# A fused retention and Mish-MLP kernel on one core: the first tile's q and k in pair loads with products in place of transposes

## The chip, the cores and the metric

The kernel runs on one NeuronCore of one Trainium2 chip. The metric is the device time of one execution in microseconds, as a median over runs. Engines are named PE (TensorE), ACT (ScalarE), DVE (VectorE), POOL (GpSimd) and SP (SyncE). SP's queue issues loads and stores without a cast; POOL's queue issues loads that may cast f32 to bf16 on the way.

## What is computed

For 8 batches of 8 heads with 576 tokens of 64 elements, a retention: scores of q and k, scaled and multiplied by a decay that depends on the head and on the distance of two tokens, zero where the key comes later, and then multiplied by v. The result, laid out as 4608 tokens of 512 elements, goes through a two-layer network whose activation is Mish.

```python
scores = scale * np.matmul(q, k.transpose(0, 1, 3, 2))
Dmat = np.where(rel >= 0, gamma[:, None, None] ** rel[None, :, :], 0.0)
ret = scores * Dmat[None, :, :, :]
attn = np.matmul(ret, v)
x = attn.transpose(0, 2, 1, 3).reshape(B * S, H * D)
h = x @ w_in                       # [4608, 512] @ [512, 2048]
g = h * np.tanh(np.log1p(np.exp(h)))
out = g @ w_out                    # [4608, 2048] @ [2048, 512]
```

All inputs and the output are f32 in DRAM; the kernel computes products in bf16 with f32 sums.

## The kernel before

The tokens are cut into 36 chunks of 128, four to a tile, so there are nine tiles of 512 tokens. Tiles 0 and 1 hold the first chunk of each batch (batches 0 to 3, and 4 to 7), which need no running state. For every tile, `g1` forms one 128-wide slice of h with four products of 512 columns and ACT applies Mish to it (16 slices a tile), and `g2` multiplies by w_out. PE works its instructions off in the order in which they are written; the whole order is written out by hand, and each engine keeps it. Attention work of later tiles is put between the products of earlier ones. Only tile 0 has nothing to hide behind: its attention is the opening, from the start to the first `g1` product.

The opening, and the names that the change touches:

- **Loads of q and k.** In tiles 0 and 1 a partition holds eight consecutive tokens of one head (16 groups of eight tokens times 8 heads are 128 partitions, 512 elements each), so that one DRAM row is 2 KB long. `load_first_qk(t, i, b)` (line 100) loads one batch from POOL's queue with a cast to bf16. For tile 0, q of batches 0 and 1 is instead loaded by SP's queue in f32 to `q0` (lines 118 and 119) and cast by DVE (lines 510 and 511). The order on POOL's queue is k of batches 0 and 1, then, after the setting up of the distance matrix and the positions, k and q of batches 2 and 3, then v of all four batches in two loads (`load_first_v`), then w_in in pieces of 256, 256 and 512 columns (`load_w_in`, line 84). The two last pieces of 512 columns are issued later, behind the casts of v that POOL does (lines 521 and 530).
- **Transposes.** `f_transpose(t, g, i, parts)` (line 179) works on two batches, g = 0 or 1, and on q (i = 0) or k (i = 1). For tile 0 it makes 16 PE transposes (a token slot r out of eight, times two batches x) of 64 columns of the loaded tile with all 128 partitions, eight to a PSUM tile, and two evictions (`parts` names the PSUM pool and the engine of each) bring them to `qkT`, with the slots interleaved back into token order. Tile 1 first mixes the two batches with DVE (`f_mix`) and makes eight transposes.
- **Scores, v, outputs.** `f_scores(0, g)` makes 16 products and four masked evictions by DVE (line 217). `f_v` casts v to bf16 with the engine that it is given. `f_out(0, b, engine)` makes 8 products and one eviction to `xT`, which `g1` reads.
- **Warmers.** `keep_warm(n)` issues n products of zeros, whose result is not used.
- **Behind the opening.** POOL goes on with tile 1's q and k, w_out and `f_state`; `f_mix` and `f_transpose(1, 0, ...)` follow the 64 products of `g1(0, ...)`.

The written order of the opening (lines 510 to 533) stands in the listing.

Of the kernel before, what the change touches and what calls it, by code (L numbers as in the profile page):

```python
# [9 lines left out]
F32 = mybir.dt.float32  # L10
BF16 = mybir.dt.bfloat16
# [5 lines left out]
def kernel(  # L17
# [18 lines left out]
    nc = tc.nc  # L36
    B, H, S, D = q.shape
    assert (B, H, S, D) == (8, 8, 576, 64)
    P = 128
    NP = H // 2  # L40
    d_model = H * D
    d_ff = moe_w_in.shape[1]
    nF = d_ff // P
# [22 lines left out]
    tr = ctx.enter_context(tc.tile_pool(name="tr", bufs=4))  # L66
# [4 lines left out]
    ps_sc = ctx.enter_context(tc.tile_pool(name="ps_sc", bufs=2, space=PS))  # L71
    ps_st = ctx.enter_context(tc.tile_pool(name="ps_st", bufs=1, space=PS))
    ps_h = ctx.enter_context(tc.tile_pool(name="ps_h", bufs=2, space=PS))
# [10 lines left out]
    def load_w_in(f0, n):  # L84
        nc.gpsimd.dma_start(out=w_in_t[:, :, ds(f0, n)], in_=w_in_r[:, :, ds(f0, n)])
# [7 lines left out]

    stage = gp.tile([P, nF, NCH * P], BF16, name="gT")
    gts = {0: gp.tile([P, nF, NCH * P], BF16, name="gT")}
    q0 = gts[0][:, H:nF, :].bitcast(F32).rearrange("p (b a) c -> p b (a c)", a=2)
    v0 = {}
    fst = {}

    def load_first_qk(t, i, b):  # L100

        name = ("qb", "kb")[i]
        if t not in fst:
            fst[t] = {"qb": stage[:, 0:4, :], "kb": stage[:, 4:8, :], "vb": {}}
        nc.gpsimd.dma_start(out=fst[t][name][:, b, :],  # L105
                            in_=(q, k)[i][4 * t + b, :, 0:P, :].rearrange("h (g r) d -> g h (r d)", r=8))

    def load_first_v(b):

        if b < 4:  # L110
            pair = stage[:, ds(8 + 2 * b, 4), :].bitcast(F32).rearrange("p a (c d) -> p (a c) d", d=D)
        else:
            pair = first.tile([P, 2 * H, D], F32, name="vpair", bufs=2)
        for e in range(2):
            v0[b + e] = pair[:, ds(H * e, H), :]
        nc.gpsimd.dma_start(out=pair, in_=v[ds(b, 2), :, 0:P, :].rearrange("b h p d -> p (b h) d"))  # L116

    for b in range(2):
        nc.sync.dma_start(out=q0[:, b, :], in_=q[b, :, 0:P, :].rearrange("h (g r) d -> g h (r d)", r=8))
    for b in range(2):  # L120
        load_first_qk(0, 1, b)

    zeros = consts.tile([P, 512], BF16)
    nc.vector.memset(zeros, 0.0)
# [7 lines left out]
    ident = consts.tile([P, P], BF16)  # L132
# [3 lines left out]
    nc.gpsimd.iota(pos[64:P, 4:5], pattern=[[1, 1]], base=512, channel_multiplier=1,  # L136
                   allow_small_or_imprecise_dtypes=True)
    for i in (1, 0):
        for b in (2, 3):
            load_first_qk(0, i, b)  # L140
    load_first_v(0)
    load_first_v(2)
    for f0, n in ((0, 256), (256, 256), (512, 512)):
        load_w_in(f0, n)
    mask = consts.tile([P, P], F32)
    mask2 = consts.tile([P, P], F32)
# [13 lines left out]
    def keep_warm(n, pool=ps_o, name="ops"):  # L160
        idle = pool.tile([P, 512], F32, name=name)
        for _ in range(n):
            nc.tensor.matmul(idle, lhsT=zeros[:, 0:P], rhs=zeros, start=True, stop=True)
# [8 lines left out]
    def f_mix(g, i):  # L172
# [3 lines left out]
        nc.vector.tensor_copy(fst[1][name, "mix", g].rearrange("p r x d -> p x r d"),  # L176
                              fst[1][name][:, ds(2 * g, 2), :].rearrange("p x (r d) -> p x r d", r=8))

    def f_transpose(t, g, i, parts):

        name = ("qb", "kb")[i]
        out_t = tr.tile([P, 2, NP, P], BF16, name="qkT", bufs=5).rearrange("p i n t -> p (i n) t")
        n = 8 // len(parts)
        moves = []
        for j, (pool, tname, copy) in enumerate(parts):
            tp = pool.tile([P, 2, 8, P] if tname == "sc" else [P, 8, P], BF16, name=tname)
            tp = (tp[:, 0] if tname == "sc" else tp)[:, 0:n]
            for r in range(n):
                if t == 1:
                    mix = fst[1][name, "mix", g][:, n * j + r]  # L190
                    nc.tensor.transpose(tp[:, r, :], mix.rearrange("p x d -> p (x d)"), ident)  # L191
                else:
                    for x in range(2):
                        nc.tensor.transpose(tp[ds(64 * x, 64), r, :],
                                            fst[0][name][:, 2 * g + x, ts(n * j + r, D)], ident)
            moves.append((copy, out_t.rearrange("p h (g r) -> p h g r", r=8)[:, :, :, ds(n * j, n)],
                          tp.rearrange("p r (g h) -> p h g r", h=H)))
        for copy, to, src in moves:
            copy(to, src)
        fst[t][name, g] = out_t  # L200

    def f_scores(t, g):

        qT, kT = fst[t]["qb", g], fst[t]["kb", g]
        scs = [ps_sc.tile([P, 2, NP, P], F32, name="sc") for _ in range(2)]
        for x in range(2):
            fst[t]["sm", 2 * g + x] = first.tile([P, H, P], BF16, name="sm0", bufs=4)
        for hs in (0, NP):
            for h in range(hs, hs + NP):
                for x in range(2):  # L210
                    r = ds(64 * x, 64)
                    to = scs[hs // NP][:, x, h - hs, :] if t == 0 else scs[x][:, hs // NP, h - hs, :]
                    nc.tensor.matmul(to, lhsT=kT[r, h, :], rhs=qT[r, h, :], start=True, stop=True)
            for x in range(2):
                sm = fst[t]["sm", 2 * g + x]
                if t == 0:
                    nc.vector.tensor_tensor(sm[:, ds(hs, NP), :], scs[hs // NP][:, x], dmask[:, ds(hs, NP), :],
                                            op=OP.mult)
                elif hs > 0:
                    nc.vector.tensor_tensor(sm, scs[x].rearrange("p a b i -> p (a b) i"), dmask, op=OP.mult)  # L220

    def f_v(t, b, copy):
        vb = first.tile([P, H, D], BF16, name="vb", bufs=4)
        copies = copy if isinstance(copy, tuple) else (copy,)
        n = H // len(copies)
        for j, copy in enumerate(copies):
            copy(vb[:, ds(n * j, n), :], v0[4 * t + b][:, ds(n * j, n), :])
        fst[t]["vb"][b] = vb

    def f_out(t, b, copy):  # L230
        if b == 0:
            xts[t] = xp.tile([P, KC, NCH * P], BF16, name="xT")
        vb = fst[t]["vb"][b]
        if t == 0:
            pool, name = ((ps_h, "hp"), (ps_h, "hp"), (ps_st, "st"), (ps_o, "ops"))[b]
            ot = pool.tile([P, NP, P], F32, name=name)
        else:
            ot = ps_sc.tile([P, 2, NP, P], F32, name="sc")[:, 0]
        for p in range(NP):
            for e in range(2):  # L240
                nc.tensor.matmul(ot[ds(64 * e, 64), p, :], lhsT=vb[:, 2 * p + e, :],
                                 rhs=fst[t]["sm", b][:, 2 * p + e, :],
                                 start=(p == 0), stop=True, skip_group_check=True)
        copy(xts[t][:, :, ts(b, P)], ot)
# [256 lines left out]
    dve, act, pool = nc.vector.tensor_copy, nc.scalar.copy, nc.gpsimd.tensor_copy  # L501
# [5 lines left out]
    nc.scalar.activation(gq, ex, AX.Exp)  # L507
    nc.scalar.activation(gv, ex, AX.Exp, scale=-1.0)
    nc.scalar.activation(warm, lnd, AX.Mish)
    for b in range(2):  # L510
        dve(fst[0]["qb"][:, b, :], q0[:, b, :])
    keep_warm(12)
    f_transpose(0, 0, 1, [(ps_h, "hp", act), (ps_h, "hp", dve)])
    f_transpose(0, 0, 0, [(ps_st, "st", act), (ps_o, "ops", dve)])
    keep_warm(2, ps_sc, "sc")
    f_transpose(0, 1, 1, [(ps_h, "hp", act), (ps_h, "hp", act)])
    f_scores(0, 0)
    f_transpose(0, 1, 0, [(ps_st, "st", act), (ps_o, "ops", act)])
    for b in range(2):
        f_v(0, b, pool)  # L520
    load_w_in(1024, 512)
    keep_warm(3, ps_h, "hp")
    f_scores(0, 1)
    keep_warm(3)
    f_out(0, 0, act)
    f_out(0, 1, act)
    keep_warm(4, ps_st, "st")
    f_v(0, 2, dve)
    f_v(0, 3, (act, pool))
    load_w_in(1536, 512)  # L530
    f_out(0, 2, dve)
    f_out(0, 3, act)
    keep_warm(2, ps_sc, "sc")
    for i, b in ((1, 0), (1, 1), (0, 0), (0, 1)):
        load_first_qk(1, i, b)
# [9 lines left out]
    for b in (4, 6):  # L545
        load_first_v(b)
# [17 lines left out]
    for i in range(nF):  # L564
        for step in steps.get(i, "").split():
            n = int(step[1])
# [27 lines left out]
    for u in range(24):  # L594
        j, w = divmod(u, 4)
# [33 lines left out]
    for t in range(2, nT + 1):  # L629
        for i in range(nF):  # L630
            n, w = NCH * (t + 1) + i // 8 * 2, i % 8
# [84 lines left out]
```

## Time and profile before

| | |
|---|---|
| runs before | 305.67 us median of 3 (305.58 to 305.85) |
| the profiled execution | 305.06 us |
| its span in the profile | 303.3 us, 6347 instructions |
| opening: first product of g1 (line 435) | at 16.60 us |
| the 64 products of g1 for tile 0 | 16.60 to 30.83 us |
| data moved | 47.35 MB, mean 156 GB/s; HBM read 38.80 MB |

The 40 slices of the span show the shape of the run (each digit is a busy share in tenths):

```profile
PE   7899999999999999999999999999999999999996
DVE  4713546678969737363666463636271511011011
ACT  5556227883466534334343333434433333333200
POOL 8786857847966465561939392716210000000000
DMA  7999999999999969699999896979322100010131
```

PE is short of nine tenths in the first two slices (to 15.2 us) and in the last. The DMA engines are at nine tenths for more than half of the run. The groups of loads that concern the opening (queue, count, KB each, median time from issue to landing; for a casting load the KB are those written):

```profile
w_in_t<-in_moe_w_in_dram POOLq DMA_DIRECT2D x3, 512.0 KB, 10.5
gT<-in_k_dram POOLq DMA_DIRECT2D x8, 128.0 KB, 6.3
gT<-in_v_dram POOLq DMA_DIRECT2D x2, 512.0 KB, 7.0
gT<-in_q_dram POOLq DMA_DIRECT2D x6, 128.0 KB, 8.6
gT<-in_q_dram SPq DMA_DIRECT2D x2, 256.0 KB, 3.9
w_in_t<-in_moe_w_in_dram POOLq DMA_DIRECT2D x2, 256.0 KB, 8.0
```

`gT` is the name of the buffer that the opening borrows for its loads.

### The profile page before, as it was taken

How to read it: one execution, taken by the hardware profiler on the slowest of the kernel's cores; microseconds unless marked ns; L12 is line 12 of the kernel's file. 1: busy time of each engine (PE TensorE's matmuls, PEld its weight loads, DVE VectorE, ACT ScalarE, POOL GpSimd, SP SyncE). 2: the span in 40 equal slices, each digit the busy share in tenths (PEclk: the TensorE clock that was granted, in tenths of full speed). 3: DMA queues.
4: the chain of work that ended last, by engine and by line, in shares of the span. 5: the costliest groups of instructions: out<-in, count | busy, mean ns of one | idle time of the engine just before them, and what ended most of it. 6: DMA issues, size and time to landing. Idle time of an engine off the chain costs nothing.

```text
span 303.3 us, 6347 instructions
## 1 busy us (share of the span) xinstructions
PE 297.0 (98%) x2682; PEld 147.4 (49%) x2682; DVE 143.8 (47%) x225; ACT 130.3 (43%) x227; POOL 138.7 (46%) x186
## 2 busy tenths in 40 slices
PE   7899999999999999999999999999999999999996
PEld 3444555556455545454545454545454544444443
DVE  4713546678969737363666463636271511011011
ACT  5556227883466534334343333434433333333200
POOL 8786857847966465561939392716210000000000
PEclk9999999999999999999999999999999999999999
DMA  7999999999999969699999896979322100010131
GB/s 152 211 204 205 205 237 247 325 216 213 243 249 246 216 115 217 139 165 196 193 160 204 180 223 128 190 156 164 81 72 69 37 37 35 35 37 36 40 100 69
DMA packets 39613, 47.35 MB, mean 156 GB/s; under 512 B 21792, under 2 KB 28448, under 8 KB 39584
## 3 DMA queue, kind: packets, MB, share of 16 engines
q0 software_dynamic: 14896, 32.25, 51.4%
q1 hardware_dynamic: 24544, 14.49, 22.3%
q8 instruction: 21, 0.34, 0.5%
q10 hardware_dynamic: 144, 0.20, 0.2%
q14 instruction: 8, 0.07, 0.1%
HBM read 38.80 MB, written 9.44 MB: 159 GB/s over the span
## 4 chain that ended last, share of the span: by engine, by line
PE 92%; DMA 3%; POOL 3%; issue 0%; DVE 0%; POOLq 0%
PE hp L435 40%; PE ops L450 32%; DMA w_in_t<-in_moe_w_in_dram 3%; PE hp L450 3%; PE hp L467 2%; PE sc L317 2%; PE hp L388 2%; PE st L354 2%; PE hp L404 2%; PE sc L303 1%; PE st L467 1%; PE ops L467 1%; PE hp L479 1%; POOL gT L105 1%; POOL gT L116 1%; PE sc L191 1%
## 5 line engine op out<-in xcount | busy, mean ns | idle before, releaser
L435 PE MATMUL hp<-xT,w_in_t 128*128 128x512 bf16 x576 | 137.1, 379 | 0.2
L437 ACT ACTIVATE gT<-hp 128x512 bf16<-128x512 f32 x144 | 86.0, 598 | 104.3 <-PE hp L435 104.0
L450 PE MATMUL ops<-w_out_t,gT 128*128 128x512 bf16 x448 | 110.2, 380 | 0.0
L435 PEld LDWEIGHTS <-w_in_t 128*128 128x128 bf16 x576 | 55.7, 98 | 66.8 <-issue 1.1
L450 PEld LDWEIGHTS <-gT 128*128 128x128 bf16 x496 | 47.4, 98 | 56.3 <-issue 0.3
L487 DVE COPY res<-ops 128x512 f32<-128x512 f32 x29 | 20.0, 691 | 88.2 <-PE ops L450 87.8
L287 DVE TENSOR_TENSOR qks<-qkraw,gqk 128x512 bf16<-128x512 f32 x56 | 39.1, 742 | 3.5 <-DMA qkraw<-in_k_dram 3.5
L416 POOL COPY held<-qkT 128x1 bf16<-128x1 bf16 x18 | 5.9, 325 | 60.6 <-DMA qkT<-qks 60.6
L321 DVE TENSOR_TENSOR sm<-sc,mask 128x1024 bf16<-128x1024 f32 x28 | 32.9, 1215 | 0.0
L271 POOL DMA_DIRECT2D qkraw<-in_q_dram x24 | 21.3, 888 | 4.7 <-DMA vpair<-in_v_dram 1.5
L271 POOL DMA_DIRECT2D vraw<-in_v_dram x24 | 21.4, 890 | 3.3 <-DMA vpair<-in_v_dram 1.5
L271 POOL DMA_DIRECT2D qkraw<-in_k_dram x24 | 21.2, 883 | 2.3 <-DMA w_out_t<-in_moe_w_out_dram 0.7
L294 POOL TENSOR_TENSOR vs<-vraw,gv 128x512 bf16<-128x512 f32 x18 | 18.9, 1076 | 4.9 <-PE hp L388 4.8
L410 ACT CAST xT<-hp 128x512 bf16<-128x512 f32 x13 | 7.6, 585 | 26.8 <-PE hp L404 26.8
L368 DVE TENSOR_TENSOR total<-st,total 128x256 f32<-128x256 f32 x16 | 6.8, 424 | 12.8 <-issue 5.4
L304 ACT COPY qkT<-sc 128x1024 bf16<-128x1024 bf16 x10 | 10.1, 1015 | 5.2 <-PE sc L303 5.2
L410 DVE CAST xT<-hp 128x512 bf16<-128x512 f32 x14 | 9.6, 685 | 4.1 <-PE hp L404 3.7
L450 PE MATMUL hp<-w_out_t,gT 128*128 128x512 bf16 x48 | 11.0, 379 | 0.0
L467 PEld LDWEIGHTS <-gT 128*128 128x128 bf16 x64 | 5.8, 98 | 6.5
L376 ACT CAST ssb<-total 128x256 bf16<-128x256 f32 x24 | 8.9, 408 | 0.3 <-DVE total L366 0.2
L317 PE MATMUL sc<-qkT 64*64 64x128 bf16 x448 | 8.7, 217 | 0.0
L388 PE MATMUL hp<-sm,vs 128*64 128x128 bf16 x216 | 8.6, 220 | 0.0
(107 smaller groups left out, 219.3 us busy)
## 6 DMA issues: line engine op xcount, KB each, us to landing
out_dram<-res SPq DMA_DIRECT2D x31, 256.0 KB, 3.6
qkraw<-in_q_dram POOLq DMA_DIRECT2D x24, 256.0 KB, 7.8
qkraw<-in_k_dram POOLq DMA_DIRECT2D x24, 256.0 KB, 8.0
vraw<-in_v_dram POOLq DMA_DIRECT2D x24, 256.0 KB, 8.7
w_out_t<-in_moe_w_out_dram POOLq DMA_DIRECT2D x4, 512.0 KB, 11.3
k0r<-in_k_dram POOLq DMA_DIRECT2D x8, 256.0 KB, 5.2
w_in_t<-in_moe_w_in_dram POOLq DMA_DIRECT2D x3, 512.0 KB, 10.5
gT<-in_k_dram POOLq DMA_DIRECT2D x8, 128.0 KB, 6.3
```

The source lines that it names most:

```text
L271: nc.gpsimd.dma_start(out=t, in_=src[b, :, ds(P * c, P), :].rearrange("h p d -> p h d"))
L287: nc.vector.tensor_tensor(slots[:, :, y], heads[:, :, y], factors[:, :, y].unsqueeze(3).to_broadcast([P, NP, 2, D]), op=OP.mult)
L294: engine.tensor_tensor(vs, live[n]["v"], gv[:, c, :].unsqueeze(2).to_broadcast([P, H, D]), op=OP.mult)
L317: nc.tensor.matmul(sc[j, e, p, :], lhsT=qk[r, 1, p, j], rhs=qk[r, 0, p, :], start=True, stop=True, skip_group_check=True)
L321: nc.vector.tensor_tensor(sm.rearrange("p e n i -> p (e n) i"), sc.rearrange("p e n i -> p (e n) i"), m.unsqueeze(1).to_broadcast([P, 2 * ...
L388: nc.tensor.matmul(both[h % 2][ds(64 * a, 64), h // 2, ts(x, P)], lhsT=vs[:, 2 * h + a, :], rhs=sm[:, h % 2, 2 * (h // 2) + a, :], start=( ...
L410: copy(xts[t].rearrange("p (h e) i -> p e h i", e=2)[:, e, :, ds(P * s, 2 * P)], both[e])
L435: nc.tensor.matmul(hp, lhsT=w_in_t[:, c, ts(f, P)], rhs=xts[t][:, c, :], start=(c == 0), stop=(c == KC - 1))
L437: nc.scalar.activation(gts[t][:, f, :], hp, AX.Mish)
L450: nc.tensor.matmul(ops, lhsT=gts[t][:, f, ts(s, P)], rhs=w_out_t[:, f, :], start=(f == 0), stop=(f == nF - 1))
L467: nc.tensor.matmul(outs[0, s], lhsT=gts[0][:, f, ts(s, P)], rhs=w_out_t[:, f, :], start=(f == 0), stop=(f == nF - 1))
L487: copy(ot, ops)
```

## The change

Five things change, all in tile 0's opening.

1. q and k of tile 0 are loaded two batches at a time by a new `load_pair(i, g)`, from POOL's queue with the cast: k of batches 0 and 1, q of batches 0 and 1, then, after the same setting up, k and q of batches 2 and 3. A partition now holds sixteen consecutive tokens (8 groups of sixteen tokens times 16 pairs of batch and head), 1024 elements, so a DRAM row is 4 KB long. SP's two loads, `q0` and DVE's two casts are gone. Six loads of POOL's queue become four.
2. A new `f_transpose_pair` replaces the 16 transposes of a call by 32 products with 64 columns: the loaded tile's 64 columns of one token slot (sixteen slots) are the stationary side, and half of the identity, the 64 columns that belong to batch x, is the moving side. Each of the two PSUM tiles has eight slots in f32 instead of four in bf16, and is evicted by one copy as before. The first k call is evicted by DVE twice instead of ACT and DVE.
3. w_in comes in pieces of 256, 256, 256, 256, 512 and 512 columns, all issued ahead of POOL's casts of v.
4. The order of the first part: nine warmers instead of twelve, two more after the first k call, and the scores of batches 0 and 1 ahead of the second k call instead of behind it.
5. v of batch 2 is cast by ACT and POOL in halves and of batch 3 by DVE (the other way round before), and the evictions of batches 2 and 3 to `xT` are ACT's and DVE's (DVE's and ACT's before).

```diff
-    q0 = gts[0][:, H:nF, :].bitcast(F32).rearrange("p (b a) c -> p b (a c)", a=2)
...
+    def load_pair(i, g):
...
+        nc.gpsimd.dma_start(out=fst[0][("qb", "kb")[i]][:, ds(2 * g, 2), :].rearrange("p x c -> p (x c)"),
+                            in_=(q, k)[i][ds(2 * g, 2), :, 0:P, :].rearrange("b h (g r) d -> g (b h) (r d)", r=16))
...
-    for b in range(2):
-        nc.sync.dma_start(out=q0[:, b, :], in_=q[b, :, 0:P, :].rearrange("h (g r) d -> g h (r d)", r=8))
-    for b in range(2):
-        load_first_qk(0, 1, b)
+    for i in (1, 0):
+        load_pair(i, 0)
...
     for i in (1, 0):
-        for b in (2, 3):
-            load_first_qk(0, i, b)
+        load_pair(i, 1)
     load_first_v(0)
     load_first_v(2)
-    for f0, n in ((0, 256), (256, 256), (512, 512)):
+    for f0, n in ((0, 256), (256, 256), (512, 256), (768, 256), (1024, 512), (1536, 512)):
         load_w_in(f0, n)
...
+    def f_transpose_pair(g, i, parts):
+
+        name = ("qb", "kb")[i]
+        rows = fst[0][name][:, ds(2 * g, 2), :].rearrange("p x c -> p (x c)")
+        cols = ident.rearrange("p (g x h) -> p x g h", x=2, h=H)
+        out_t = tr.tile([P, 2, NP, P], BF16, name="qkT", bufs=5).rearrange("p i n t -> p (i n) t")
+        moves = []
+        for j, (pool, tname, copy) in enumerate(parts):
+            tp = pool.tile([P, 8, D], F32, name=tname)
+            for r in range(8):
+                for x in range(2):
+                    nc.tensor.matmul(tp[ds(64 * x, 64), r, :], lhsT=rows[:, ts(8 * j + r, D)], rhs=cols[:, x],
+                                     start=(r == 0), stop=True, skip_group_check=True)
+            moves.append((copy, out_t.rearrange("p h (g r) -> p h g r", r=16)[:, :, :, ds(8 * j, 8)],
+                          tp.rearrange("p r (g h) -> p h g r", h=H)))
...
     def f_transpose(t, g, i, parts):
 
+        if t == 0:
+            return f_transpose_pair(g, i, parts)
...
-    for b in range(2):
-        dve(fst[0]["qb"][:, b, :], q0[:, b, :])
-    keep_warm(12)
-    f_transpose(0, 0, 1, [(ps_h, "hp", act), (ps_h, "hp", dve)])
+    keep_warm(9)
+    f_transpose(0, 0, 1, [(ps_h, "hp", dve), (ps_h, "hp", dve)])
+    keep_warm(2, ps_sc, "sc")
     f_transpose(0, 0, 0, [(ps_st, "st", act), (ps_o, "ops", dve)])
     keep_warm(2, ps_sc, "sc")
+    f_scores(0, 0)
     f_transpose(0, 1, 1, [(ps_h, "hp", act), (ps_h, "hp", act)])
-    f_scores(0, 0)
     f_transpose(0, 1, 0, [(ps_st, "st", act), (ps_o, "ops", act)])
     for b in range(2):
         f_v(0, b, pool)
-    load_w_in(1024, 512)
     keep_warm(3, ps_h, "hp")
...
-    f_v(0, 2, dve)
-    f_v(0, 3, (act, pool))
-    load_w_in(1536, 512)
-    f_out(0, 2, dve)
-    f_out(0, 3, act)
+    f_v(0, 2, (act, pool))
+    f_v(0, 3, dve)
+    f_out(0, 2, act)
+    f_out(0, 3, dve)
```

More of the change, by code (lines that the diff above doesn't have):

```diff
@@ L106, in load_first_qk @@
                             in_=(q, k)[i][4 * t + b, :, 0:P, :].rearrange("h (g r) d -> g h (r d)", r=8))
+    def load_pair(i, g):
+        if 0 not in fst:
+            fst[0] = {"qb": stage[:, 0:4, :], "kb": stage[:, 4:8, :], "vb": {}}
+        nc.gpsimd.dma_start(out=fst[0][("qb", "kb")[i]][:, ds(2 * g, 2), :].rearrange("p x c -> p (x c)"),
+                            in_=(q, k)[i][ds(2 * g, 2), :, 0:P, :].rearrange("b h (g r) d -> g (b h) (r d)", r=16))
     def load_first_v(b):
@@ L177, in f_mix @@
                               fst[1][name][:, ds(2 * g, 2), :].rearrange("p x (r d) -> p x r d", r=8))
+    def f_transpose_pair(g, i, parts):
[12 more added lines that the diff above has]
+                          tp.rearrange("p r (g h) -> p h g r", h=H)))
+        for copy, to, src in moves:
+            copy(to, src)
+        fst[0][name, g] = out_t
     def f_transpose(t, g, i, parts):
+        if t == 0:
+            return f_transpose_pair(g, i, parts)
         name = ("qb", "kb")[i]
@@ L188, in f_transpose @@
             for r in range(n):
[L189 to L195, printed above, removed]
+                mix = fst[1][name, "mix", g][:, n * j + r]
+                nc.tensor.transpose(tp[:, r, :], mix.rearrange("p x d -> p (x d)"), ident)
             moves.append((copy, out_t.rearrange("p h (g r) -> p h g r", r=8)[:, :, :, ds(n * j, n)],
```

## The prediction

> **What bounds the kernel now.** I read the busy totals first, then the chain of waits, then the opening in the timeline, then the landings of single loads.
>
> ```profile
> PE 297.0 (98%) x2682; PEld 147.4 (49%) x2682; DVE 143.8 (47%) x225; ACT 130.3 (43%) x227; POOL 138.7 (46%) x186
> ```
> TensorE is busy for 297.0 of 303.3 us. The question is where the missing 6.3 us lie. The stages (TensorE's time is the first number after the length):
>
> ```profile
> 0.00:16.60 16.60, 13.40 (x154) 6.64 (x155) 10.47 (x35) 9.14 (x16) 13.12 (x26) 1.00 0.96 182
> 16.60:30.83 14.23, 14.15 (x67) 6.33 (x68) 2.40 (x2) 8.96 (x15) 10.12 (x15) 1.00 1.24 205
> 30.83:60.00 29.17, 29.17 (x265) 15.09 (x263) 16.87 (x23) 15.19 (x25) 21.00 (x27) 1.00 1.10 255
> ```
> After 30.83 us TensorE doesn't pause until the tail. So the change, which lies wholly in the opening, is worth what it moves the start of an unbroken product stream, and no more. The chain of waits for that place (start, length, what):
>
> ```profile
> 5.79 2.47 POOL gT L116 x2
> 8.26 1.47 POOL w_in_t L85 x2
> 9.73 10.52 DMA w_in_t<-in_moe_w_in_dram
> 20.25 0.05 issue
> 20.29 10.53 PE hp L435 x48
> ```
> The fifth group of four g1 products (0.865 us a group) starts at 20.29, when the third w_in load lands. Counted back by four groups, 20.29 - 3.46 = 16.83 us is where the stream starts in effect, although the first product is at 16.60: the load costs 0.23 us. What holds 16.60 itself is in the timeline (start, length, engine, line):
>
> ```profile
> 7.35 0.57 ACT L199 COPY qkT<-hp 128x512 bf16<-128x512 bf16 x1
> 8.46 0.62 PE L213 MATMUL sc<-qkT 64*128 64x128 bf16 x16
> 10.25 0.41 PE L194 MATMUL st<-ident,gT 128*64 128x128 bf16 x7 [0.81 <-DMA gT<-in_q_dram]
> 11.18 0.59 ACT L199 COPY qkT<-ops 128x512 bf16<-128x512 bf16 x1
> 12.26 2.48 DVE L217 TENSOR_TENSOR sm<-sc,dmask 128x512 bf16<-128x512 f32 x4 [0.81 <-PE sc L213]
> 14.67 0.56 DVE L227 CAST vb<-gT 128x512 bf16<-128x512 f32 x1
> 15.96 0.58 ACT L244 CAST xT<-ops 128x512 bf16<-128x512 f32 x1 [1.00 <-PE ops L241]
> 16.60 3.61 PE L435 MATMUL hp<-xT,w_in_t 128*128 128x512 bf16 x16
> ```
> The last q load lands (10.25), is transposed, copied by ScalarE until 11.77, scored, masked on VectorE for 2.48 us, then v's cast, f_out, xT, g1. From the end of ScalarE's last copy to g1 it is 16.60 - 11.77 = 4.83 us, all serial.
>
> Landings (issue plus time to landing of single issues, in the view of DMA issues): k0 4.8, k1 6.1, q0 4.3, q1 5.9, k2 6.7, k3 7.75, q2 9.1, q3 10.26, v pairs 12.24 and 14.5, w_in 15.4, 17.7, 20.25, then 22.8 and 25.4; tile 1's k, k, q, q 26.0 to 27.9.
>
> **The change, part by part.**
>
> *The loads.* A casting pair load reads 512 KB and writes 256 KB. No such load is in the trace. Nearest rows: w_in's 1 MB read lands 2.55 us after the one before (17.7 to 20.25), and tile 1's 256 KB reads land 0.65 us apart, so 1.27 to 1.3 us a pair. The far end is the opening itself: k1 at 6.1 to q3 at 10.26 is 1 MB in 4.16 us, 2.1 us a pair. I take 1.27: tile 1's loads have the old opening loads' very form and ran at it, and the opening's slowness looks like supply. From 7 to 8 us the software queue's share is 90.9% with 0.14 MB moved, from 17 to 18 us it is 124.0% with 0.21 MB, and between 5 and 8 us no packet is over 2 KB, so v's are not there, though v is issued at 5.74. POOL now saves two issues there: kp1 and qp1 at 3.54 and 4.1, v from 4.7 instead of 5.74 (L105 takes 0.55 us each, if rows of double length cost no more).
>
> The software queue's first bytes come after 3.0 us (before that only the other queue moves), and k0 landed some 0.8 us behind its bytes. So: first k pair 3.0 + 1.27 + 0.8 = 5.1, q pair 6.35, second k pair 7.6, q pair 8.9. At the far end: 5.9, 8.0, 10.1, 12.1. v follows at 2.0 and 2.26 us a pair as before: 10.9 to 11.1 and 13.2, by 1.2 us earlier; with nothing gained, 14.5.
>
> *SP's loads and the casts removed.* Q of batches 0 and 1 moves from SP's queue (issued 0.81) behind k on POOL's. Nothing else stood on SP there. VectorE loses two casts (0.42 and 0.43 us), which puts it at k's copies early.
>
> *The products.* Four calls of 16 transposes of 128 columns become 32 products of 64 columns. The same form is in the trace:
>
> ```profile
> L354 PE MATMUL st<-vs,qks x160: 195/196/218, 59.0 to 239.0; 128*64 128x64 bf16 x160
> ```
> There 24 in a row occupy 73.96 to 74.36, 17 ns each; 32 make 0.54 us, where 16 transposes take 0.44 (0.64 less 0.2 us of latency). That is +0.1 us a call; the first two are hidden behind ScalarE's table load (until 7.23) and its next small activation. The evictions are as many, of 512 elements; sources of f32 cost the same (L244: 0.69 on VectorE, 0.58 on ScalarE; L199: 0.69 and 0.57 to 0.60).
>
> *Warmers.* Nine at 0.42 us from 1.26 end at 5.04, just ahead of k at 5.1.
>
> *The opening's path.* k's products 5.1 to 5.65, its two copies on VectorE 5.65 to 7.0. q's products 6.4 to 6.95; ScalarE can copy from 7.35 to 7.94, VectorE from 7.2 to 7.9. Scores at 8.0 (8.46 before). Scores now stand ahead of the second k pair on TensorE: its products start at 8.45, ScalarE's four copies at 9.0; at 0.52 apart the last ends at 11.15 (11.77 before). q's second pair must be there by 9.6 not to hold this; it lands at 8.9. Scores 11.2, VectorE 11.65 to 14.13, v's cast to 14.65 (v needed by 14.1, there at 13.2). Batch 2's f_out now goes first and only batch 3's follows the cast: cast end to xT start 0.51 us as before, xT 0.69 on VectorE, g1 0.06 later: 15.9.
>
> *w_in.* POOL issues all six at 0.75 us from 7.2 to 11.7, before f_v; f_v waited until 12.38 for v before, and v is due at 11.1, so POOL delays it to 11.7 at most and still ends it at 12.9, not 13.55. The trace has eight software loads in flight: the 18th waits for the 10th (w_out at 18.01 for the w_in that lands at 17.7), the 19th for the 11th. So issues 9 to 12 wait for the four pairs, landed by 8.9; w_out for the third and fourth w_in pieces (about 18 and 19.5). The queue is backed up until 27 us, so none starves it. Each quarter piece takes 1.27 us, or 1.6 (the first two land 3.2 us after v). Landings 16.5, 17.8 to 18.1, 19.1 to 19.7, 21.6 to 22.3, 24.2 to 24.8 against needs at 17.6, 19.4, 21.1, 22.8, 26.3: no wait. If the q and k loads gain nothing, the piece at 1024 (22.8 to 23.5) would hold the stream at 15.9 to 16.5.
>
> *What is late next.* Tile 1's first transposes (TensorE at 30.66) need VectorE's mixing, done at 30.05 and 30.38, behind q's landing at 27.9. That is 0.5 us of slack, plus what the load stream gains (0.5 to 1.2).
>
> *Sum.* 16.83 - 15.9 = 0.9 us off the profiled execution's 305.06 (span 303.3 and 1.8 around it). That execution is 0.61 under the median of the runs, 305.67, so the median should be **304.8**. The path can't gain more than about 1.0 us: ScalarE's table load fixes 7.35. It ends at a gain of 0.3 where v lands at 14.5 as before.
>
> **Rivals.**
>
> 1. *A pair load is carried by half of the engines.* Then 512 KB take 2.55 us; k and q go side by side on the two halves: 3.0 + 2.55 + 0.8 = 6.35 and 7.0, then 8.9 and 9.5. k's copies on one engine become the path: 6.9 to 8.2, q's half on VectorE to 8.95, scores 9.0, ScalarE's copies 10.0 to 12.1, g1 at 16.8 to 16.9: the whole gain is the vanished w_in wait, and the time is 305.7 (305.3 to 306.2). Every load in this trace has 16 or more rows outermost, so no row speaks to it; the new source has 8.
> The Trainium skill (DMA: Bandwidth & Descriptors, "Why a DMA increments its semaphore by 16 and not by 1") has just this rule: the largest count up to 16 that divides both sides' slowest dimension, here 8; no run here shows it yet.
>
> 2. *Slower: the opening's own rate stays* (2.1 us a pair). q's second pair lands at 12.1; ScalarE ends 1.5 later (10.26 to 11.77 before), 13.6, and g1 starts at 13.6 + 4.72 = 18.3: 1.5 us lost, 307.2. It decides from a landing at 10.6 on. For it: four loads of this trace did so. Against: the supply argument above.
>
> 3. *The stream of loads gains nothing and the quarter pieces cost 0.3 us each.* Tile 1's q is 0.65 late, the mixing ends at 31.0, and the transposes take the gain back: 305.5.
>
> **How the numbers follow.** My sum 0.45, half the engines 0.30, slow loads 0.15, the stream 0.10. What a measurement here can tell from no change is about 0.2%, 0.61 us. My sum's own range is 304.5 to 305.4, of which 0.38 is under 305.06. Faster: 0.38 plus 0.02 of rival 1. Slower: all of rival 2 and 0.06 of rival 1. Same: the rest, 0.39. The range 304.4 to 306.4 leaves out most of rival 2.
>
> **What would show it.** Right: k lands near 5.1 and q's second pair before 9.6; scores near 8.0; the first g1 product near 15.9 and 64 of them without a wait. Wrong: k at 6.3 with q beside it (rival 1); pairs landing 2 us apart (rival 2); g1 early but idle ahead of tile 1's transposes (rival 3). A product call of over 0.7 us, or a copy on VectorE of over 0.75, would undo the middle of the sum.

## The result, and the profile after

The changed kernel takes 308.11 us (median of 4 runs, 307.63 to 308.48); the kernel before, beside it, 305.62 us (304.6 to 305.85). The ratio is 1.0085, with an interval of 1.0060 to 1.0109: slower by some 2.5 us, where 304.8 was forecast with a range up to 306.4. The profiled execution of the changed kernel took 308.48 us with a span of 306.8, the highest of its four runs.

The busy totals and the stages of the changed kernel, cut as those of before (start and end, length, then busy time and number of instructions of TensorE, its weight loads, VectorE, ScalarE and POOL, the granted clock, DMA share, GB/s):

```profile
PE 294.0 (96%) x2707; PEld 148.1 (48%) x2745; DVE 143.5 (47%) x224; ACT 130.3 (42%) x226; POOL 137.3 (45%) x185
```

```profile
0.00:16.60 16.60, 12.29 (x195) 6.59 (x198) 9.22 (x31) 7.44 (x13) 11.60 (x22) 0.90 0.82 140
16.60:30.83 14.23, 12.37 (x70) 5.53 (x70) 1.96 (x6) 8.10 (x15) 8.99 (x14) 1.00 1.31 202
```

(TensorE's 294.0 is a little low: its matmul records are 2707 beside 2745 weight loads, where before had 2682 of each.) In the first 16.6 us the DMA engines moved 140 GB/s where they had moved 182, and the clock was 0.90. The second stage, which was full of products before, now has 1.9 us without any: the stream starts inside it. The opening in the timeline (start, length, engine, line; in brackets the idle time before it and what ended it):

```profile
6.73 0.69 PE L193 MATMUL hp<-ident,gT 128*64 128x64 bf16 x32 [1.45 <-DMA gT<-in_k_dram]
8.41 0.44 PE L193 MATMUL st<-ident,gT 128*64 128x64 bf16 x16 [0.45 <-DMA gT<-in_q_dram]
10.16 1.04 PE L232 MATMUL sc<-qkT 64*128 64x128 bf16 x16
11.52 0.95 PE L193 MATMUL hp<-ident,gT 128*64 128x64 bf16 x32 [0.32 <-DMA gT<-in_k_dram]
14.75 2.48 DVE L236 TENSOR_TENSOR sm<-sc,dmask 128x512 bf16<-128x512 f32 x4 [1.37 <-PE sc L232]
20.37 13.97 PE L454 MATMUL hp<-xT,w_in_t 128*128 128x512 bf16 x63 [0.34 <-DVE gqk L572]
```

The products wait three times for pair loads. The four pairs landed at 6.69, 8.37, 11.48 and 12.37 us, the two v pairs at 14.58 and 18.20. The stream of g1 products starts at 20.37 and then doesn't pause: the wait for w_in that stood ahead of the fifth group is gone. The chain of waits for that place (start, length, what):

```profile
4.92 1.16 POOL gT L122
6.08 12.12 DMA gT<-in_v_dram
18.20 0.02 issue
18.22 0.41 ACT vb L246
18.64 0.04 issue
18.68 0.58 PE st L260 x8
```

Both v loads had been issued by 7.3 us, so what held the start were loads, from the first one to the last. From the first g1 product to the end of the span it is 306.8 - 20.37 = 286.4 us; before, from the effective start, it was 303.3 - 16.83 = 286.5. In these two executions the whole loss is made by the time that the stream starts; e11 and e12 show below that a second limit stands close behind it.

### The profile page after: what moved, and what is told of

Read it like the earlier page. It is cut to its first block, busy times and chain, and to the rows that moved or that the text cites. A ratio compares the mean times of both kernels' runs of the same rounds, so it can differ in the third digit from the quotient of the medians.

```text
span 306.8 us, 6426 instructions
## 1 busy us (share of the span) xinstructions
PE 294.0 (96%) x2707; PEld 148.1 (48%) x2745; DVE 143.5 (47%) x224; ACT 130.3 (42%) x226; POOL 137.3 (45%) x185
## 4 chain that ended last, share of the span: by engine, by line
PE 91%; DMA 4%; issue 2%; POOL 1%; DVE 0%; ACT 0%; POOLq 0%
PE hp L454 40%; PE ops L469 31%; DMA gT<-in_v_dram 4%; PE hp L469 3%; PE hp L486 2%; PE sc L336 2%; PE hp L407 2%; PE st L373 2%; PE hp L423 2%; PE sc L322 1%; PE ops L486 1%; PE hp L498 1%; PE st L486 1%; POOL gT L111 1%; PE sc L214 1%
## 5 line engine op out<-in xcount | busy, mean ns | idle before, releaser
L469 PE MATMUL ops<-w_out_t,gT 128*128 128x512 bf16 x434 | 107.0, 379 | 2.1 <-issue 2.1
L306 DVE TENSOR_TENSOR qks<-qkraw,gqk 128x512 bf16<-128x512 f32 x56 | 38.2, 726 | 2.6 <-DMA qkraw<-in_k_dram 2.6
L435 POOL COPY held<-qkT 128x1 bf16<-128x1 bf16 x18 | 4.8, 269 | 62.0 <-DMA qkT<-qks 62.0
```

What stands on the lines that cost most here:

```text
L306: nc.vector.tensor_tensor(slots[:, :, y], heads[:, :, y], factors[:, :, y].unsqueeze(3).to_broadcast([P, NP, 2, D]), op=OP.mult)
L469: nc.tensor.matmul(ops, lhsT=gts[t][:, f, ts(s, P)], rhs=w_out_t[:, f, :], start=(f == 0), stop=(f == nF - 1))
```

## The experiments

"Span less start" is the span minus the start of the first g1 product (before: the effective 16.83). All numbers but the medians and ratios are of the profiled execution. Median of before beside them: 305.29 to 305.62 us.

| kernel | median us (runs) | ratio to before, interval | first g1 | span less start |
|---|---|---|---|---|
| changed kernel | 308.11 (4) | 1.0085, 1.0060 to 1.0109 | 20.37 | 286.4 |
| sixteen rows outermost (e1) | 306.46 (4) | 1.0046, 1.0031 to 1.0061 | 18.32 | 286.4 |
| half engines in before (e2) | 307.20 (4) | 1.0065, 1.0043 to 1.0086 | 19.12 | 286.3 |
| changed, w_in as before (e3) | 307.91 (4) | 1.0089, 1.0074 to 1.0104 | 19.93 | 286.6 |
| w_in pieces in before (e4) | 305.45 (10) | 1.0006, 0.9993 to 1.0018 | 16.63 | 286.6 |
| more PE instructions in before (e5) | 305.79 (11) | 1.0009, 0.9989 to 1.0029 | 16.54 | 286.7 |
| e1, ten warmers fewer (e6) | 306.85 (11) | 1.0054, 1.0034 to 1.0073 | 18.45 | 286.5 |
| e1, q by SP (e7) | 305.07 (11) | 0.9990, 0.9973 to 1.0007 | 16.83 | 286.7 |
| before, q by POOL (e8) | 307.00 (11) | 1.0052, 1.0036 to 1.0068 | 19.04 | 286.4 |
| e7, evictions as before (e9) | 305.21 (12) | 0.9995, 0.9984 to 1.0006 | 16.57 | 286.7 |
| e1, more PE instructions (e10) | 306.51 (5) | 1.0049, 1.0032 to 1.0065 | 18.40 | 286.4 |
| changed, more PE instructions (e11) | 308.13 (4) | 1.0093, 1.0080 to 1.0106 | 18.93 | 287.3 |
| changed, clock held (e12) | 308.48 (5) | 1.0098, 1.0084 to 1.0111 | 19.55 | 287.2 |

### How many engines carry a load: e1 and e2

The changed kernel's pair load has 8 rows outermost on both sides. In e1 the 16 pairs of batch and head stand outermost instead, and only the order of the partitions differs, which the columns of the identity and the view of the eviction take up:

```diff
-                            ....rearrange("b h (g r) d -> g (b h) (r d)", r=16))
+                            ....rearrange("b h (g r) d -> (b h) g (r d)", r=16))
-        cols = ident.rearrange("p (g x h) -> p x g h", x=2, h=H)
+        cols = ident.rearrange("p (x i) -> p x i", x=2)
-                          tp.rearrange("p r (g h) -> p h g r", h=H)))
+                          tp.rearrange("p r (h g) -> p h g r", h=H)))
```

> The changed kernel with one thing altered: batch and head, 16 of them, are the outermost dimension of a pair load's source instead of the 8 groups of sixteen tokens; rows are still 4 KB, products as many. Theory (a pair load with 8 outermost is carried by half of the engines): all 16 engines carry it, the pairs land near 5.2, 6.5, 7.8 and 9.1 us instead of 6.7, 8.4, 11.5 and 12.4, the first g1 product comes near 16.0 instead of 20.4, and the time is 304.6 to 305.5 us. Rival (4 KB rows or two pair loads behind each other are slow in themselves): the pairs land within 0.5 us of where the changed kernel has them and the time is 307.5 to 308.5.

e2 does the opposite in the kernel before: its loads of q and k of tile 0, SP's too, get the 8 heads outermost, and nothing else changes.

```diff
-                            in_=(q, k)[i][4 * t + b, :, 0:P, :].rearrange("h (g r) d -> g h (r d)", r=8))
+                            in_=(q, k)[i][4 * t + b, :, 0:P, :].rearrange(
+                                "h (g r) d -> h g (r d)" if t == 0 else "h (g r) d -> g h (r d)", r=8))
...
-        nc.sync.dma_start(out=q0[:, b, :], in_=q[b, :, 0:P, :].rearrange("h (g r) d -> g h (r d)", r=8))
+        nc.sync.dma_start(out=q0[:, b, :], in_=q[b, :, 0:P, :].rearrange("h (g r) d -> h g (r d)", r=8))
...
-                          tp.rearrange("p r (g h) -> p h g r", h=H)))
+                          tp.rearrange("p r (h g) -> p h g r" if t == 0 else "p r (g h) -> p h g r", h=H)))
```

> The kernel before with its own loads of 2 KB rows, but the 8 heads outermost in the source of tile 0's q and k loads instead of the 16 groups of tokens; nothing else of the change. Theory (half engines): no engine pair works evenly, the last q of tile 0 lands at 11.5 to 12.5 us instead of 10.3, v later by as much, and the time is 306.5 to 308 us. Rival (the row length or the pairing is what slowed the changed kernel): no change, 305.3 to 305.9.

A load's completion count rises by one sixteen times in the trace; the text takes each rise as the word of one DMA engine that it is done. The times of these rises for the first k pair load, in us:

```
changed kernel   3.19 3.20 3.21 3.22 3.23 3.25 3.26 3.29   6.42 6.44 6.45 6.52 6.53 6.54 6.66 6.69
```

Eight engines are done early and the other eight 3.2 us later. What the early eight had to do is in the packets of the first 3 us of the changed kernel (view of DMA):

```profile
DMA packets 144, 0.02 MB, mean 6 GB/s; under 512 B 136, under 2 KB 136, under 8 KB 144
```

136 packets are of 4 bytes and last 7 ns each; 8 carry data. Of the q pair's count, eight come at 6.60 to 6.87, just behind k's data, and eight at 8.14 to 8.37: as if q's data went over the half that k had left idle (the counts don't name their engines). In e1 all sixteen counts of the first load come between 4.70 and 5.39. The products of e1 (timeline):

```profile
5.43 0.93 PE L193 MATMUL hp<-ident,gT 128*64 128x64 bf16 x32
8.92 0.69 PE L193 MATMUL hp<-ident,gT 128*64 128x64 bf16 x32
10.85 0.44 PE L193 MATMUL st<-ident,gT 128*64 128x64 bf16 x16 [1.24 <-DMA gT<-in_q_dram]
18.32 2.97 PE L454 MATMUL hp<-xT,w_in_t 128*128 128x512 bf16 x13 [0.34 <-DVE gqk L572]
```

The first transposes start 1.3 us sooner, the stream 2.05 us sooner, and the time falls by 1.65 us (308.11 to 306.46). In e2 the trace again shows 136 packets of 4 bytes and eight early counts, k's first products wait, and the time rises by the ratio 1.0065:

```profile
7.01 0.24 PE L195 MATMUL hp<-ident,gT 128*64 128x128 bf16 x1 [1.11 <-DMA gT<-in_k_dram]
8.34 0.94 PE L195 MATMUL hp<-ident,gT 128*64 128x128 bf16 x15 [1.08 <-DMA gT<-in_k_dram]
```

So eight rows outermost cost time in either kernel, and e2's time is where it was expected. But e1's time (306.46) lies between its two forecasts and above before's: the engines are one part of the loss only.

### w_in in smaller pieces: e3 and e4

e3 is the changed kernel with w_in's pieces and their places as before; e4 is the kernel before with the changed kernel's six early pieces (256 four times, 512 twice).

```diff
-    for f0, n in ((0, 256), (256, 256), (512, 256), (768, 256), (1024, 512), (1536, 512)):
+    for f0, n in ((0, 256), (256, 256), (512, 512)):
...
+    load_w_in(1024, 512)
...
+    load_w_in(1536, 512)
```

> The changed kernel with w_in in pieces of 256, 256, 512, 512, 512 columns, the last two issued behind POOL's casts of v, as before the change. Theory (q and k loads make the loss): the time stays at 307.6 to 308.5. Rival (the early w_in pieces, whose issue waits for the pairs on POOL, or share engines with v, make a good part of the loss): 307.3 or less.

> The kernel before with w_in alone in pieces of 256, 256, 256, 256, 512, 512 columns, all issued ahead of POOL's casts of v. Theory: the wait of 0.23 us ahead of the fifth group of g1 goes, 305.2 to 305.6. Rival (small pieces cost more of the load stream than they give): 305.8 or more.

e3 stands at 1.0089 where the changed kernel stands at 1.0085, and e4's interval holds 1: the pieces neither cost nor save anything that can be told from no change. e4 also shows that the wait for w_in was worth little: its first product is at 16.63 and its stream has no pause, against 16.83 effective before, and the time didn't follow.

### Which queue brings q: e7, e8 and e9

e8 makes one step of the change alone, in the kernel before: q of batches 0 and 1 goes over POOL's queue with a casting load, and SP's two loads and VectorE's two casts are gone.

```diff
-    for b in range(2):
-        nc.sync.dma_start(out=q0[:, b, :], in_=q[b, :, 0:P, :].rearrange("h (g r) d -> g h (r d)", r=8))
-    for b in range(2):
-        load_first_qk(0, 1, b)
+    for i in (1, 0):
+        for b in range(2):
+            load_first_qk(0, i, b)
...
-    for b in range(2):
-        dve(fst[0]["qb"][:, b, :], q0[:, b, :])
```

> The kernel before with q of batches 0 and 1 loaded by POOL's casting queue behind k, in its own form of 2 KB rows with 16 outermost; SP's two loads and VectorE's two casts are gone. This is the move to the other queue alone. Theory: the stream starts 0.9 us later, the last q and v land 0.3 to 0.8 us later, the time is 305.6 to 306.2. Rival (less written, two casts fewer): 304.8 to 305.2.

e7 takes that step back in e1: SP loads the first q pair in two halves as float32, and VectorE casts them.

```diff
-    for i in (1, 0):
-        load_pair(i, 0)
+    for j in range(2):
+        nc.sync.dma_start(out=q0[:, j, :],
+                          in_=q[0:2, :, 0:P, :].rearrange("b h (g r) d -> (b h) g (r d)", r=16)[:, :, ts(j, 512)])
+    load_pair(1, 0)
...
+    for j in range(2):
+        dve(fst[0]["qb"][:, j, :], q0[:, j, :])
```

> The kernel with 16 rows outermost (e1), but q of batches 0 and 1 by SP's queue in f32 in two halves of eight token slots and cast by VectorE, as before the change. Theory (SP's queue moves bytes from 2.0 us, POOL's from 2.9, and the load stream is full until 30 us): the last q of tile 0 and v land 0.4 to 0.9 us earlier than in e1 (10.8 and 16.2) and the time is 305.5 to 306.1. Rival (the f32 rows cost the write side what the early start gives): 306.3 to 306.7.

e8 loses 1.6 us (ratio 1.0052), and e7 gains 1.4 us on e1 (306.46 to 305.07). The direction is the forecast one, the size is about double in both: e8's last q lands 1.5 us later than before's (11.73) and its v 1.6 us later (16.11), where 0.3 to 0.8 was expected. What the queues had moved by 5.0 us is in the view of DMA (queue and kind: packets, MB, share of 16 engines over the window). Before:

```profile
q1 hardware_dynamic: 287, 0.52, 36.8%
q0 software_dynamic: 184, 0.17, 21.2%
```

The changed kernel:

```profile
q0 software_dynamic: 218, 0.17, 29.0%
```

e1, and then e8:

```profile
q0 software_dynamic: 185, 0.35, 46.7%
```

```profile
q0 software_dynamic: 328, 0.30, 48.4%
```

And e7:

```profile
q0 software_dynamic: 142, 0.26, 30.5%
q1 hardware_dynamic: 189, 0.35, 22.0%
```

q1 is SP's queue, q0 POOL's. The bytes are those written, and POOL's casting loads read twice what they write. So by 5 us the kernel before had read 0.52 + 0.34 = 0.86 MB, e7 0.35 + 0.52 = 0.87, e1 0.70, e8 0.60, and the changed kernel 0.34. Ranked by that they are ranked by their times: 305.1 (e7) and 305.6, which can't be told apart, 306.5 (e1), 307.0 (e8), 308.1. (An order of five kernels suggests a cause and doesn't show it; what shows it is e7 and e8.) SP's queue starts its first packet at 2.29 us, and POOL's at 2.73 in e1 and e8 and at 3.19 before, where the two filled the engines side by side. In e8 POOL also issues two loads more, so that v is issued at 6.78 instead of 5.74; in e1 v is issued at 4.74 and the loss is there all the same, so late issues alone aren't the cause. In e1 one engine ends v 1.0 us behind the others (16.16), which may be part of e1's 1.4; e8 has no such engine (its v ends at 16.11, the fifteenth engine at 15.77), and the loss is there.

e9 puts the evictions and v casts of the last two batches in e7 as they were before:

```diff
-    f_v(0, 2, (act, pool))
-    f_v(0, 3, dve)
-    f_out(0, 2, act)
-    f_out(0, 3, dve)
+    f_v(0, 2, dve)
+    f_v(0, 3, (act, pool))
+    f_out(0, 2, dve)
+    f_out(0, 3, act)
```

> e7 with the last part of the change undone: v of batch 2 cast by VectorE and of batch 3 by ScalarE and POOL in halves, f_out of batch 2 evicted by VectorE and of batch 3 by ScalarE. In e7 all three casts start together at 14.7 us when v lands, so the halves end last and the last eviction is VectorE's 0.69 us. Theory: the first g1 product comes 0.2 to 0.4 us earlier than e7's 16.8, the time is 304.5 to 304.9 against before's 305.3. Rival (the stream of loads or tile 1's transposes hold it anyway): 305.0 to 305.3, as e7.

Both are within their intervals of before and of each other (0.9990 and 0.9995): neither order of the casts can be called better, and neither kernel beats before by more than its interval. In e9's profile the first g1 product did come 0.26 us sooner (16.57), as expected; the time didn't follow, as its rival had it.

e7 also says what the rest of the change is worth. It has the pair loads, the products, the w_in pieces and the new order, with all engines and SP's queue for q, and equals before. Its last q load lands at 10.19 us and its v at 14.64, against 10.21 and 14.50: merging the loads brought them no sooner.

### The clock: e12

In the changed kernel the granted clock fell behind the longer waits (windows of 1 us; the clock is the third number from the end):

```profile
9.00:10.00 1.00, 0.67 (x11) 0.26 (x8) 0.69 (x1) 0.48 (x1) 1.00 (x2) 0.50 1.09 199
10.00:11.00 1.00, 1.00 (x17) 0.77 (x16) 0.11 (x1) 0.00 (x0) 0.27 (x1) 0.50 1.20 248
```

Sixteen score products took 1.04 us there against 0.62 before. e12 issues 17 warm-up products instead of 9 ahead of the first transposes:

```diff
-    keep_warm(9)
+    keep_warm(17)
```

> The changed kernel with seventeen first warmers instead of nine, so that TensorE works until about 6.8 us, when k lands. In the changed kernel the granted clock is 0.50 from 9 to 12 us. Theory: the clock stays at 1.00 through the opening, the products between 10 and 12.5 us take half, but q's second pair (12.4) and v (18.2) come as late as before, so the time is within 0.3 us of the changed kernel's 308.1. Rival (the slow clock is a good part of the loss): 307.5 or less.

```profile
9.00:10.00 1.00, 0.75 (x18) 0.21 (x11) 0.69 (x1) 0.57 (x1) 1.00 (x2) 1.00 1.14 205
10.00:11.00 1.00, 0.61 (x16) 0.43 (x16) 0.50 (x1) 0.00 (x0) 0.28 (x1) 1.00 1.15 240
```

The clock stayed at 1.00 and the scores took 0.62 us, yet the time is 308.48, no less than the changed kernel's. One part of the expectation missed: the second v pair landed at 16.69 us, not at 18.2, and the first g1 product came 0.82 us sooner, at 19.55. (On the way TensorE stood for 0.48 us, from 17.98 to 18.46, without a wait that the profile shows.) That gain was lost again further on, as in e11 below. So holding the clock gives nothing in the changed kernel, where a second limit stands close behind the first. In e2 and e8 the clock fell too (to 0.50 from 8.5 to 11.9 us and from 11.5 to 14.9), behind the waits for loads, and what it adds to their losses was not measured alone. In e1 and e7 it stood at 1.00, so their difference of 1.4 us is free of it.

### The last engine of v, and the instruction packet: e5, e6, e10 and e11

In the changed kernel fifteen engines finish the second v pair by 16.84 us and one at 18.20. From 15.5 to 17.5 us the view of DMA has, beside the loads, one packet of another queue (16 KB; 4.2% of 16 engines over 2 us is 1.34 us of one engine):

```profile
q0 software_dynamic: 684, 0.37, 132.7%
q8 instruction: 1, 0.02, 4.2%
```

It starts at 15.76. In e1 such a packet runs at 13.71, and its v pair ends at 16.16, one engine behind the others (15.15); before it runs at 15.10, behind v. The theory: the change's additional TensorE instructions bring the fetch of the next block of instructions forward into v's load. Four kernels are to move it. e5, e10 and e11 put many narrow products in place of the warm-up products ahead of the first transposes: 78 for 12 in before, and 58 for 9 in e1 and in the changed kernel, as here:

```diff
-    keep_warm(9)
+    idle = ps_o.tile([P, 512], F32, name="ops")
+    for _ in range(58):
+        nc.tensor.matmul(idle[0:32, 0:80], lhsT=zeros[:, 0:32], rhs=zeros[:, 0:80], start=True, stop=True)
```

e6 drops ten warm-up products of e1:

```diff
-    keep_warm(2, ps_sc, "sc")
...
-    keep_warm(2, ps_sc, "sc")
...
-    keep_warm(3, ps_h, "hp")
...
-    keep_warm(3)
```

> The kernel before; its first twelve warmers of 512 columns are cut into 78 of 80 columns on 32 weight columns, about as long in all. TensorE has 66 more instruction pairs ahead of f_out, as the changed kernel has. Theory (what the half engines don't explain is a fetch of 16 KB of TensorE's instructions: it takes one DMA engine for 0.9 to 1.3 us, and more instructions bring it from behind v's second load to ahead of it): the instruction queue shows its first packet before 14 us instead of 15.1, v's second pair lands 0.8 to 1.4 us later than 14.5, and the time is 306.0 to 306.8. Rival (the fetch is harmless or its place doesn't hang on the count): 305.2 to 305.7.

> The kernel with 16 rows outermost (e1) less ten warmers: the two behind each of the first k and q calls and the two times three around the second scores. Theory of the fetch: it moves behind v's second load or well into its end; v lands at 15.0 to 15.4 instead of 16.2 and the time falls from 306.4 to 305.3 to 305.8. Rival (the fetch isn't what holds v): 306.2 to 306.7. If the clock falls for want of warmers, the granted clock shows it and the time is over 306.7.

> The kernel with 16 rows outermost (e1), its first nine warmers cut into 58 of 80 columns on 32 weight columns: 49 more instruction pairs of TensorE, for nothing. Theory of the fetch: the 16 KB packet of the instruction queue comes before 11 us instead of at 13.7, early enough for its engine to catch up as in e5, v lands at 15.0 to 15.5 instead of 16.2, and more instructions make the kernel faster: 305.3 to 305.9 against 306.4. Rival (the fetch doesn't hold v): 306.3 to 306.7.

> The changed kernel with the same cut of its first warmers. Theory of the fetch: its packet moves from 15.8 us to before 13, v lands at 16.8 to 17.2 instead of 18.2, time 306.8 to 307.5 against 308.1. Rival: 307.8 to 308.5.

e5 moved the packet to 8.14 and changed nothing (1.0009; second v pair at 14.56), where the theory had 306.0 to 306.8. e6 missed: the packet stayed at 13.81, and with fewer warm-up products the clock fell to 0.61 between 13 and 17 us. e10 moved it to 10.22, where it fell on the first v pair (14.09 instead of 12.97); the second came at 15.81 instead of 16.16, with one engine still 0.91 us behind the others (14.90), and the time is the same (306.51 to 306.46). e11 moved it to 10.27; the second v pair came at 16.59, 1.6 us sooner, and the first g1 product at 18.93, 1.44 us sooner, and yet the time is 308.13. Where this went is in the timeline of e11, in tile 1's stage:

```profile
67.11 1.02 PE L454 MATMUL hp<-xT,w_in_t 128*128 128x512 bf16 x4 [0.68 <-ACT gT L456]
```

TensorE pauses for 0.68 us, because ScalarE stood for 0.62 us until a load of k0r landed:

```profile
65.03 0.62 ACT L277 CAST k<-k0r 128x512 bf16<-128x512 f32 x1 [0.62 <-DMA k0r<-in_k_dram]
```

In the changed kernel that cast runs at 65.62 and neither engine waits. TensorE had come 1.3 us sooner to this stage (its g1 products there start at 51.16 instead of 52.46). The load had been issued 0.65 us sooner (54.91 instead of 55.56), but it landed at 65.01, where the changed kernel has 65.05, and from there on e11 is 0.58 us ahead (71.14 to 70.56). The profiled execution of the changed kernel was its slowest, by 0.3 to 0.9 us of span; whether an engine was late in the others is not on record. So one engine's delay of v holds the first g1 product in the changed kernel's profile, but taking it away gave back none of the median time.

What took the gain is a second limit: the stream of loads on POOL's queue. The chain of waits in e11 runs through it (start, length, what):

```profile
22.63 12.11 DMA w_out_t<-in_moe_w_out_dram
39.74 11.54 DMA vraw<-in_v_dram
54.91 10.10 DMA k0r<-in_k_dram
```

e12 lost its 0.82 us in the same way: the cast waited for k0r until 65.15, and TensorE paused for 0.31 us at 67.23 and for 0.26 us at 165.40. In the kernel before, the same load and cast are these:

```profile
52.98 0.88 POOL L254 DMA_DIRECT2D k0r<-in_k_dram  x1 [0.28 <-DMA qkraw<-in_k_dram]
62.27 0.61 ACT L258 CAST k<-k0r 128x512 bf16<-128x512 f32 x1
```

It lands 9.25 us after its issue, at 62.23, 0.04 us ahead of the cast. So already before the change the loads were all but late there, and an earlier start without earlier loads would have gained next to nothing. That agrees with e4, whose first product came 0.2 us sooner and whose time did not. In the changed kernel this load is 2.8 us later than before. That alone is as much as the loss of 2.5 us, so in its executions without a late engine the loads, and not the first g1 product, may well set the time.

Does the packet make an engine late? The completion counts speak for it. In the kernel before, the packet runs from 15.10 to 15.99 us; the w_in load that lands at 15.46 has its last count 0.08 us behind the fifteenth, and the next three have it 0.93, 0.88 and 0.91 us behind, about the packet's length. In e12 it runs at 15.72, nearly as in the changed kernel, and v's last count comes 0.02 us behind the fifteenth; the gap, 0.75 us, shows in the w_in load behind v. So the time at which it runs doesn't alone decide whether v is hit, and which engine it falls on isn't on record. The theory that the number of TensorE's instructions sets its place held for e5, e10 and e11; in e6, with ten products fewer than e1, it stayed.

## Why the prediction was wrong

**What held.** The frame did in part: after the opening TensorE has no pause, and the span follows the start of the stream, at 286.3 to 286.7 us, in all but two profiles (e11, e12). Those two show what it left out. It named tile 1's first transposes as what is late next, with 0.5 us of slack; the load of k0r, with 0.04 us, was closer. The products cost what was taken (32 of them: 0.58 us of weight loads, 0.69 us with the latency), the copies of float32 0.59 to 0.69 us, the masks 2.48. The w_in wait vanished, and the pieces cost nothing (e3, e4). The eight loads in flight are seen again: the issue of the eleventh load, w_in at 11.76 us, waited 1.49 us, until the third, a k pair, had landed at 11.48. Tile 1's first transposes found their slack as said.

**The first step that failed** is the first of the loads: "I take 1.27" for a pair, from first bytes at 3.0. The first pair was to land at 5.1 and landed at 6.69. Rival 1's mechanism is true: half of the engines carry such a load (e1, e2, and the counts). It was mis-sized, though, and less in the first load (forecast at 6.35, landed at 6.69) than behind it: q beside it was to land at 7.0 and landed at 8.37, and the second pairs, at 8.9 and 9.5, landed at 11.48 and 12.37. As it kept the rest of the sum, the rival gave g1 at 16.9 and 305.7 us. Measured alone, eight outermost rows for sixteen cost 1.65 us (e1).
The Trainium skill (DMA: Bandwidth & Descriptors, "Why a DMA increments its semaphore by 16 and not by 1") says that the engines of a load are the largest number up to 16 that divides the slowest dimension on both sides, that on GpSimd's queue all 16 add one whatever the shape, and that the engines are taken in rotation. The trace agrees with the first two: sixteen counts, eight at 3.2 us and eight at 6.4 to 6.7. The rotation fits q's counts, eight at 6.60 to 6.87 and eight at 8.14 to 8.37, but no count names its engine.

**The second is the step costed at nothing**: "Q of batches 0 and 1 moves from SP's queue behind k on POOL's. Nothing else stood on SP there." That was the reason for a price, not against one: nothing else stood there, so nothing takes its place. SP's queue had brought 0.52 of the 0.86 MB read by 5 us, beside POOL's. The step alone costs 1.6 us (e8) and taking it back gives 1.4 (e7). The sum moved 512 KB from one queue behind another and left the pace of the second as it was.

**The third is the pace of the second pairs**: "the opening's slowness looks like supply". (The slow rate was itself read a little high: by the completion counts k1 landed at 6.25 and q3 at 10.21, so 2.0 us a pair and not 2.1.) With all engines (e1) the first two pairs came 1.23 us apart, as forecast, at 5.39 and 6.62; but the next two came at 8.53 and 10.81, 1.9 and 2.3 us apart, though POOL had issued the last of them and the first v load by 6 us. So the argument against rival 2 falls: the loads were there, and the pace was still low, 135 GB/s from 7 to 8 us before and 135 in e1. e1's last landing (10.81) lies past the point from which rival 2 was to decide (10.6), and its g1 start, 18.32, is the rival's 18.3. That agreement is luck: the rival had q's second pair hold it, from 12.1, and in e1 v's last engine held it, from 16.16. Why the queue is slow from 6.5 to 9 us stays open.

**What followed.** v stands behind the pairs on the same queue: forecast at 11.0 and 13.2, landed at 14.58 and 18.20. The last masks end at 14.75 + 2.48 = 17.23 where 14.13 was forecast, 3.1 us late; v's last engine adds the rest, 20.37 against 15.9 for g1. So the range failed as the rivals were priced one at a time, each beside a sum that was otherwise right: half engines, a lost queue and the slow second pairs came together, and only one of them was in any single case.

**The account**, in medians: the kernel with pairs on all engines and q still by SP (e7) equals before; q over POOL adds 1.4 us (e1); eight rows outermost for sixteen add 1.65 us (the changed kernel).

## What to carry to other kernels

Before merging loads, look at the outermost dimension of both sides: with 8 there, half of the engines did the work, and one rearrangement to 16 gave 1.65 us back. A load that has a queue of its own in the opening isn't free to move: count what each queue has brought by the time that it is needed. When the start of a stream is to come sooner, look for the load behind it that has the least slack: here one with 0.04 us stood 46 us further on. Price the ways of being late together where they stand on one queue, as each delays all that is behind it.

## What the runs showed of the hardware

- A load with 8 rows outermost came with 136 packets of 4 bytes, 7 ns each, within the first 3 us: 17 for each of the eight engines left out, if they are spread evenly. The changed kernel and e2 have them by then, and before, e1, e7 and e8 have none.
- A float32 load of v with rows of 256 bytes wrote 4 KB packets in about 309 ns and kept 208 (e7) to 223 GB/s (e1) between 11 and 13 us; the casting pair loads wrote 2 KB packets in 173 ns.
- The clock stood at 0.50 from 8.8 to 12.2 us in the changed kernel, after TensorE had idled for 1.45 us up to 6.73 and 0.45 us up to 8.41. The Trainium skill (TensorE: Matmul & The Clock Gate, "Part 1: The HAM clock gate") has the half clock after an idle window of about 3.4 us; the level agrees, but no unbroken idle stretch of that length stands before the drop in this trace.
- In the openings one packet of the instruction queue, 16 KB, takes 0.89 to 1.34 us, and one engine's share of the loads behind it can end that much later than the others' (before: 0.88 to 0.93 us behind a packet of 0.89).
